# Zero fills and key conversions on ScalarE, and the order of issue as a literal list, in a linear-attention and long-convolution kernel

## The chip, the cores and the metric

The kernel runs on one core of a Trainium2 chip. A core has a tensor engine (PE, with its weight loads counted apart as PEld), a vector engine (DVE), a scalar engine (ACT), a GpSimd engine (POOL) and a sync engine (SP). Each takes the instructions of its own queue in the order in which they were issued; an instruction that waits holds up those behind it on its engine, and semaphores tie the engines together. Here POOL issues the loads that convert fp32 to bf16 on their way, and SP issues the plain copies, the transposing ones and the stores. The metric is the time of one execution on the device, in microseconds (us); less is better.

## The reference

Two computations follow each other. The first is linear attention with positive random features over 8 batches, 8 heads, 576 rows and 64 columns, with 128 features; the second is a gated long convolution over rows of 512 columns.

```python
def phi(x):                                   # x: q or k, times 1/sqrt(sqrt(64))
    h = einsum('bhsd,md->bhsm', x, omega) - sum(x * x, -1) / 2
    return exp(h - max(h, -1)) / sqrt(128)
q_p, k_p = phi(q_s), phi(k_s)
kv, z = einsum('bhsm,bhsd->bhmd', k_p, v), sum(k_p, axis=2)
attn = (q_p @ kv) / (q_p @ z + 1e-6)          # per batch and head

x = attn with the heads side by side           # 8 x 576 x 512
x1, x2, x3 = split(x @ w_proj)                 # w_proj 512 x 1536
conv = irfft(rfft(x2, axis=1) * rfft(filter_fft, axis=0), n=576)
out = (x1 * conv * x3) @ w_out                 # w_out 512 x 512
```

## The kernel before

**Staging.** The eight batches are worked in pairs. Of the 576 rows of a batch, 512 are the main part (4 tiles of 128) and 64 are "left" rows, which are handled for two batches at once (names ending in `l`). For each batch the keys are transposed on PE (or, from batch 5, by transposing copies on SP), multiplied by the features `om`, and put through the exponential on ACT (`ek`, `ekl`); they are then multiplied with the values (`vn`, for left rows `vcl`) into `kv`. The queries give `eqt` in the same manner. The product of `eqt` and `kv` holds numerator and denominator, and DVE divides (`rden`, `xb`). PE turns the result (`xt`, evicted by ACT) and DVE folds it along the sequence into `xf`.

The convolution of length 576 is done as a discrete Fourier transform split into three chunks of 192 rows, by matmuls with tables of sines. `project2` makes x2, `gates` (line 1250) makes x1 times x3, `forward` (1348) makes the spectrum with the tables `fwb`, `fwa`, `fwn`, `fwar` and `fwnr`, `spectrum` (1271) multiplies by the filter's spectrum `hps` and `hqs`, and the inverse (1411 and on) comes back with the tables `gtab`, `gta` and `gns`, to be added up and gated on DVE. Row halves that have to trade places go through SP copies (`sw`, `xw`). The product with `w_out` is evicted into `osb` and stored by SP in 256 KB pieces. The left rows of a pair have a gate of their own, `x13l`, made by DVE from a PE result that sits in one of the three banks of the PSUM tag `h`; the buffer `osb` has three slots, two half-sized evictions (`ya`) of the inverse also using them.

**The tables.** `make_residues` (599) makes the phases of the sines: constants by memset on DVE (`zb` holds zeros, `kc`, `ph`, `mg`), a first sine on `zb` that brings in the sine's table (`sn`), then for three sizes an activation on ACT (`yt`), a subtraction on DVE and a fused product that give the residue, whose sign bits are masked (`xt`). `sines` (668) puts them through the sine on ACT, `tables` (685) has PE transpose them, and DVE copies them out. `late_constants` (766) zeroes three buffers with DVE memsets and makes the scale `fsc`:

```python
for z in (hqs[:, 1, :], fwar[:], vcl_buf[1][:]):
    nc.vector.memset(z, 0.0)
```

**The first keys.** `first_keys` (510) has SP load the keys of batch 0 in two halves as fp32 (`ek`), and converts one half on DVE and one on ACT to bf16 (`kn`). Every other input comes by converting loads on POOL's queue: 76 of them, the projection weights (`wproj`) in three thirds of 512 KB, and a load of the next batch's keys, values or queries waits until the last reader of its buffer is done. The buffers for keys, values and queries are two deep (`kn`, `vn`, `qn`).

**What sets the order.** The whole kernel is recorded first: proxies for the engines make an `Op` of every call, consecutive matmuls into one tile being one `Op` (1348 in all). `Plan.order` (253) finds the dependences; the base time of an op is worked back from its users by latencies that `_cost` (200) gives, plus the tables `LEAD`, `SHIFT` and `LEAN` by stage, batch and engine (25 to 52). `simulate` (282) then plays the engines, the buffer slots, the load queues and PE's clock, and picks on each engine the ready op that is due first. `issue` (399) sends them all out in that order, so every instruction in the profile carries the line 405; they are told apart by tile names.

Of the kernel before, what the change touches and what calls it, by code (L numbers as in the profile page):

```python
# [24 lines left out]
PERIOD, STRETCH, STAY = 136.732, 16.038, 101.39  # L25
LEAD = {
    "cross keys": 0.92, "cross out": 7.64, "cross queries": -0.74, "filter": 4.65, "fold": -48.94,
    "forward": 107.85, "gates": -40.51, "inverse": 17.39, "keys": -0.75, "left keys": -52.95,
    "left out": -1.12, "left queries": -14.15, "load filter": 50.17, "load k": 55.36,
    "load kl": -1.11, "load q": -0.71, "load ql": 8.56, "load v": 0.49, "load vl": 1.73,  # L30
    "load w0": 1.61, "load w1": 5.28, "load w2": 1.64, "out": -42.88, "queries": 96.24,
    "residues": 1.41, "rest": 14.42, "sines": 0.5, "start": -189.65, "sums": -10.66,
    "tables": 0.2, "turn out": -3.18, "turn queries": 16.85, "values": -5.78, "zeros": 9.94,
}

SHIFT = {
    ("fold", 0): 48.94, ("fold", 1): 188.96, ("fold", 2): 50.05, ("fold", 7): 48.3,
    ("forward", 0): -112.16, ("forward", 1): -114.87, ("forward", 2): -107.32,
    ("forward", 6): -108.25, ("gates", 0): 16.24, ("gates", 1): 40.13, ("gates", 2): 50.94,
    ("gates", 6): 38.24, ("left keys", 2): 53.69, ("left keys", 6): 49.69, ("load k", 2): -56.64,  # L40
    ("load q", 0): -1.89, ("load ql", 0): -33.49, ("load v", 0): 2.07, ("load vl", 2): -6.7,
    ("queries", 1): -97.56, ("queries", 2): -131.03, ("queries", 6): -98.12,
    ("queries", 7): -93.75, ("rest", 1): 207.08, ("rest", 7): -14.42, ("turn out", 1): -12.03,
    ("turn out", 2): -153.32, ("turn queries", 1): -15.77, ("turn queries", 2): -16.64,
    ("values", 1): 546.29, ("values", 2): -24.51,
}
LEAN = {
    ("forward", "DVE"): 35.53, ("forward", "PE"): -40.96, ("gates", "DVE"): -10.03,
    ("gates", "PE"): 146.99, ("keys", "ACT"): -14.86, ("left queries", "ACT"): -47.8,
    ("queries", "ACT"): 5.49, ("queries", "PE"): 33.51, ("rest", "ACT"): -8.58,  # L50
    ("rest", "DVE"): -16.93,
}
# [33 lines left out]
class Op:  # L86
    __slots__ = (
        "eng", "calls", "reads", "writes", "due", "n", "busy", "lat", "deps", "users",
        "tiles", "start", "end", "name", "dma", "table", "where", "rows", "base",
    )  # L90

    def __init__(self, eng, due, n, name, where):
        self.eng, self.due, self.n, self.name, self.where = eng, due, n, name, where
        self.calls, self.reads, self.writes = [], [], []
        self.busy = self.lat = 0.0
        self.deps, self.users = {}, []
        self.tiles = set()
        self.dma = self.table = None
        self.rows = 128
# [13 lines left out]
class Plan:  # L113
# [4 lines left out]
    HOP = {"PE": 55.0, "DVE": 37.0, "ACT": 37.0, "POOL": 60.0, "SP": 60.0}  # L118

    def __init__(self, nc, tc):  # L120
        self.nc, self.tc = nc, tc
        self.ops, self.tile_of, self.slots = [], {}, {}
        self.where = "start", 0
        self.tensor = Proxy(self, "PE", nc.tensor)
        self.vector = Proxy(self, "DVE", nc.vector)
        self.scalar = Proxy(self, "ACT", nc.scalar)
        self.gpsimd = Proxy(self, "POOL", nc.gpsimd)
        self.sync = Proxy(self, "SP", nc.sync)
        self.allow_low_precision = nc.allow_low_precision
# [4 lines left out]
    def _new(self, eng, name):  # L134
        stage, b = self.where
        more = LEAD.get(stage, 0.0) + SHIFT.get((stage, b), 0.0) + LEAN.get((stage, eng), 0.0)
        op = Op(eng, more, len(self.ops), name, self.where)
        self.ops.append(op)
        return op

    def tile(self, pool, shape, dtype, name, bufs=1):
        t = pool.tile(shape, dtype, name=name, bufs=bufs)
        key = t.name if hasattr(t, "name") else t[:].tensor.name
        self.slots[pool.name, name] = bufs
        line = self.where[0]
        self.tile_of[key] = ((pool.name, name), "residues" if line == "load filter" else line)
        return t
# [7 lines left out]
    def record(self, eng, real, name, args, kw):  # L155
# [16 lines left out]
        if join:  # L172
            op = last
        else:
            op = self._new(eng, f"{name} {outs[0].tensor.name}")
            op.rows = ins[0].ap[0][1] if eng == "PE" else 128
# [5 lines left out]
        self._cost(op, eng, name, outs, ins)  # L182
        if name == "activation":
            op.table = {AF.Exp: "exp", AF.Sin: "sin"}.get(kw["func"])
        return op

    def opaque(self, eng, call, out, busy):
# [3 lines left out]
        op.busy = op.lat = busy  # L191

    @staticmethod
    def _free(ap):
        n = 1
        for _, c in ap.ap[1:]:
            n *= c
        return n

    def _cost(self, op, eng, name, outs, ins):  # L200
        out = outs[0]
        n = self._free(out)
        if name == "dma_start_transpose":
            op.busy, op.lat = 2000.0, 2200.0
            op.dma = ("HW", self._free(out) * 128 * 2 / 240.0)
            return
        if name == "dma_start":
            a = out if out.space != bass.MemoryType.DRAM else ins[0]
            run = a.ap[-1][1] * SIZE[a.dtype]
            rows = a.ap[0][1] * self._free(a) // a.ap[-1][1]  # L210
            if eng == "POOL":
                op.busy, op.lat = (880.0 if rows > 600 else 720.0), 3300.0
                op.dma = ("SW", rows * max(run, 166) / 198.0)
            elif out.space != bass.MemoryType.DRAM and ins[0].space == bass.MemoryType.DRAM:
                op.busy, op.lat = 580.0, 2300.0
                op.dma = ("HL", rows * run / 330.0)
            else:
                op.busy, op.lat = 580.0, 2000.0
                op.dma = ("HW", rows * run / 180.0 / (1 if out.space == bass.MemoryType.DRAM else 4))
            return  # L220
        half = all(SIZE[a.dtype] == 2 for a in (out, *ins))
        sbuf = all(a.space != bass.MemoryType.PSUM for a in (out, *ins))
        if eng == "PE":
            m = n / (4.8 if ins[0].ap[0][1] == 64 else 2.4) + 2.5
            op.lat = op.busy + n / 2.4 + 166.0
            op.busy += m
            return
        if eng == "DVE":
            if name == "memset":
                busy = n * SIZE[out.dtype] / 4.8 + 5.0  # L230
            elif name == "reciprocal":
                busy = 5.8 * n + 78.0
            elif name == "tensor_tensor":
                busy = n / (1.92 if half and sbuf else 0.96) + 68.0
            elif name == "scalar_tensor_tensor":
                busy = n / 0.96 + 130.0
            elif name in ("tensor_copy", "tensor_scalar", "tensor_scalar_mul"):
                rate = (4 if sbuf else 2) if half else (2 if sbuf else 1)
                if name != "tensor_copy" and not sbuf:
                    rate = 1  # L240
                busy = n / (0.96 * rate) + (68.0 if half else 100.0)
            elif name == "reduce_max":
                busy = self._free(ins[0]) / 0.96 + 60.0
            else:
                busy = n / 0.96 + 68.0
            op.busy, op.lat = busy, busy + 82.0
        elif eng == "ACT":
            busy = n * 0.8333 + (52.0 if not sbuf else 190.0)
            op.busy, op.lat = busy, busy + 107.0
        else:  # L250
            op.busy = op.lat = n / 1.2 + 100.0

    def order(self):
        last = {}
        for op in self.ops:
# [6 lines left out]
            for key, kind in ((op.reads, 0), (op.writes, 1)):  # L262
                for t, r in key:
                    last[t].append((op, kind, r))
                    if t in self.tile_of:
                        op.tiles.add(t)
        for op in self.ops:
            for o in op.deps.values():
                o.users.append(op)
        for op in reversed(self.ops):  # L270
            lat = op.lat + (op.dma[1] if op.dma else 0.0) + 50.0
            last = min((u.base for u in op.users), default=op.where[1] * PERIOD)
            op.base = last - STRETCH * lat / 1000.0
        for op in self.ops:
            op.due += op.base
            if op.eng == "PE":
                for u in op.users:
# [4 lines left out]
    def simulate(self):  # L282
# [8 lines left out]
        for op in ops:  # L291
            for t in op.tiles:
                left[t] = left.get(t, 0) + 1
# [1257 lines left out]
```

## Time and profile before

| | us |
|---|---|
| median of 5 runs (lowest, highest) | 267.3 (266.68, 268.03) |
| the profiled execution, own time | 269.08 |
| its span, first to last instruction | 267.0 |
| PE busy | 245.2 (92%) |
| DVE busy | 213.3 (80%) |
| ACT busy | 195.3 (73%) |
| POOL busy | 61.3 (23%) |
| mean granted PE clock | 0.987 |

A busy time is the sum over an engine's instructions. In the tables of stages that follow, an entry such as 5.83 (x58) is busy time and number of instructions. A line of the trace in order of time has the start, the length, the engine, the source line, the operation, output and input tile, their shapes and types, and the number of instructions that it joins; a bracket gives the idle time of the engine just before it and what ended that. Other groups of the page: POOL's 76 loads share one queue, which moved 16.78 MB, and SP's queue moved 19.04 MB.

### The profile page before, as it was taken

What the parts mean: (1) busy time and instruction counts of PE and PEld (TensorE: products, weight loads), DVE (VectorE), ACT (ScalarE), POOL (GpSimd) and SP (SyncE); (2) the same over time, 40 slices, a digit from 0 to 9 for tenths busy, and PEclk for the clock granted to TensorE, in tenths of its full rate; (3) what the DMA queues carried; (4) which work ended last, traced back from release to release, by engine and by line L of the source; (5) the groups of instructions that cost most, each with busy time, mean ns of one, the idle gap of its engine ahead of it and who ended that gap; (6) DMA issues with size and microseconds to landing.
All of it is one profiled execution on the core that took longest, in us unless ns stands there. A gap on an engine that the chain in (4) does not pass through costs nothing. (4 is left out here: it accounts for less than half of the span.)

```text
span 267.0 us, 5756 instructions
## 1 busy us (share of the span) xinstructions
PE 245.2 (92%) x2234; PEld 137.1 (51%) x2234; DVE 213.3 (80%) x475; ACT 195.3 (73%) x307; POOL 61.3 (23%) x86
## 2 busy tenths in 40 slices
PE   0586689999999999989999999999999999999994
PEld 0455446555476538545456454446555554456541
DVE  7999963689959999998499995979979789188470
ACT  5699479849999997986947876996495564753523
POOL 8625475444650710650031000000000000000000
PEclk9999959999999999999999999999999999999999
DMA  7999999999999999699869459525226410430406
GB/s 177 190 198 189 200 200 191 203 179 161 176 171 147 81 116 169 72 155 179 203 103 133 100 120 215 140 81 157 56 44 180 100 42 20 157 79 2 153 4 196
DMA packets 88866, 36.31 MB, mean 136 GB/s; under 512 B 60299, under 2 KB 83336, under 8 KB 88840
## 3 DMA queue, kind: packets, MB, share of 16 engines
q0 software_dynamic: 58560, 16.78, 60.9%
q1 hardware_dynamic: 30136, 19.04, 30.0%
q8 instruction: 17, 0.28, 0.4%
q10 hardware_dynamic: 144, 0.13, 0.1%
q14 instruction: 9, 0.07, 0.1%
HBM read 34.64 MB, written 9.44 MB: 165 GB/s over the span
## 5 line engine op out<-in xcount | busy, mean ns | idle before, releaser
L405 ACT CAST x<-h 128x512 bf16<-128x512 f32 x68 | 39.9, 597 | 31.2 <-PE h L405 28.2
L405 PE MATMUL h<-xt,wproj 128*128 128x512 bf16 x256 | 61.2, 380 | 0.0
L405 PEld LDWEIGHTS <-wproj 128*128 128x128 bf16 x384 | 31.2, 98 | 27.1 <-issue 2.1
L405 ACT ACTIVATE eqt<-a 128x1024 bf16<-128x1024 f32 x32 | 32.4, 1068 | 4.6 <-PE a L405 4.6
L405 ACT ACTIVATE osb<-h 128x512 f32<-128x512 f32 (+4 forms) x49 | 28.3, 577 | 8.0 <-PE h L405 6.6
L405 ACT ACTIVATE ek<-a 128x1024 bf16<-128x1024 f32 x32 | 32.3, 1048 | 0.7 <-PE a L405 0.6
L405 PE MATMUL h<-wproj,xf 128*128 128x512 bf16 x128 | 31.2, 379 | 1.2 <-DVE x13l L405 0.7
L405 PE MATMUL h<-wout,yt 128*128 128x512 bf16 x128 | 30.9, 379 | 0.3 <-DVE yt L405 0.3
L405 POOL DMA_DIRECT2D qn<-in_q_dram x26 | 22.9, 892 | 33.8 <-DMA qt<-qn 19.1
L405 DVE TENSOR_TENSOR x<-h,x 128x512 bf16<-128x512 f32 x32 | 21.8, 684 | 6.4 <-PE h L405 6.2
L405 DVE TENSOR_TENSOR bt<-h,osb 128x384 f16<-128x384 f32 x32 | 16.5, 552 | 7.8 <-PE h L405 5.3
L405 PEld LDWEIGHTS <-xf 128*128 128x128 bf16 x134 | 12.5, 99 | 14.1 <-issue 1.7
L405 PEld LDWEIGHTS <-yt 128*128 128x128 bf16 x128 | 11.9, 98 | 14.8 <-issue 0.9
L405 PE MATMUL h<-x,fwb 128*128 128x512 bf16 x72 | 18.5, 379 | 0.1
L405 PE MATMUL h<-gtab,xs 128*128 128x384 bf16 x64 | 15.6, 326 | 0.0
L405 PE MATMUL a<-om,kt 64*128 64x128 bf16 x256 | 12.1, 226 | 2.4 <-DVE kt L405 1.1
L405 PEld LDWEIGHTS <-eqt 128*128 128x128 bf16 x256 | 10.9, 98 | 5.7 <-DVE xb L405 1.3
L405 DVE TENSOR_TENSOR xb<-a,rden 128x512 bf16<-128x512 f32 x20 | 13.3, 684 | 0.4
L405 DVE TENSOR_TENSOR xf<-xt 128x1024 bf16<-128x1024 bf16 (+1 forms) x16 | 8.6, 550 | 6.3 <-ACT xt L405 6.3
L405 PE MATMUL a<-kv,eqt 128*128 128x65 bf16 x256 | 12.1, 194 | 1.0 <-DVE xb L405 1.0
L405 PE MATMUL a<-qt,om 64*128 64x512 bf16 x64 | 11.7, 397 | 1.0 <-ACT ek L405 0.7
L405 ACT CAST osb<-h 128x384 f16<-128x384 f32 x16 | 8.0, 501 | 5.9 <-PE h L405 5.3
(159 smaller groups left out, 475.7 us busy)
## 6 DMA issues: line engine op xcount, KB each, us to landing
out_dram<-osb SPq DMA_DIRECT2D x24, 256.0 KB, 2.3
vn<-in_v_dram POOLq DMA_DIRECT2D x8, 512.0 KB, 10.2
kn<-in_k_dram POOLq DMA_DIRECT2D x7, 512.0 KB, 8.7
qn<-in_q_dram POOLq DMA_DIRECT2D x24, 128.0 KB, 7.6
sw<-sp SPq DMA_DIRECT2D x16, 128.0 KB, 2.3
wproj<-in_moe_w_proj_dram POOLq DMA_DIRECT2D x3, 512.0 KB, 9.8
ek<-in_k_dram SPq DMA_DIRECT2D x2, 512.0 KB
qn<-in_q_dram POOLq DMA_DIRECT2D x2, 512.0 KB, 11.2
```

Of the source, the lines that this page charges most:

```text
L405: getattr(real, name)(*args, **kw)
```

## The change

Three things change in the code. The order of issue is no longer planned: the tables, the costs and the simulation are taken out, and `ORDER` lists the 1348 op numbers in the order in which they go out, with an assertion that no op precedes what it depends on. The two halves of the first keys are both converted on ACT. The three zeroed buffers are written on ACT by copies from the one-column tile of zeros, recorded right after the first sine, in place of the DVE memsets.

```diff
-PERIOD, STRETCH, STAY = 136.732, 16.038, 101.39
-LEAD = {
...
+ORDER = """
+    0 33 28 34 9 7 1 35 61 2 5 141 37 60 38 36 29 8 32 6 30 15 42 41 43 12 44 142 24 49 13 25 31
+    27 84 50 45 51 39 46 54 10 26 3 47 22 17 48 89 74 53 212 4 55 11 52 90 57 83 85 62 75 56 86 14
...
+    1338 1339 1343 1341 1342 1344 1345 1347 1346
+"""
...
     def order(self):
...
-        for op in self.ops:
-            op.due += op.base
...
-        return self.simulate()
-
-    def simulate(self):
...
+        order = [self.ops[int(n)] for n in ORDER.split()]
+        place = {op.n: i for i, op in enumerate(order)}
+        assert len(place) == len(order) == len(self.ops)
+        for op in order:
+            assert all(place[n] < place[op.n] for n in op.deps), "an instruction before its data"
+        return order
...
@@ first_keys
-            if g == 0:
-                nc.vector.tensor_copy(out=t_[:, hs], in_=k32[:, hs])
-            else:
-                nc.scalar.copy(out=t_[:, hs], in_=k32[:, hs])
+            nc.scalar.copy(out=t_[:, hs], in_=k32[:, hs])
@@ make_residues
         nc.scalar.activation(out=sn[:], in_=zb[:], func=AF.Sin)
+        nc.at("fills", 0)
+        for z in (
+            vcl_buf[1][:].rearrange("p j h d -> p (j h d)"),
+            hqs[:, 1, :],
+            fwar[:].rearrange("p j c -> p (j c)"),
+        ):
+            nc.scalar.copy(out=z, in_=zb[:].to_broadcast([P, z.shape[-1]]))
@@ late_constants
-        for z in (hqs[:, 1, :], fwar[:], vcl_buf[1][:]):
-            nc.vector.memset(z, 0.0)
```

The fills are 1056 columns (`vcl`), 512 (`hqs`) and 256 (`fwar`) of bf16. What the list says, against the order that the planner gave:

- **ACT** starts: first sine, fill `fwar`, fill `vcl`, `yt` of the second size, fill `hqs`, `yt` of the first size, second half of the third `yt`, one half of the key conversion, first sine of `gtab`, first half of the third `yt`, other half of the key conversion, two more sines for `gtab`, the sine for `gns`, the sine for `gta`, the exponentials. Before: first sine, `yt` of two sizes, one half of the key conversion, the third `yt`, three sines for `gtab`, those for `gns` and `gta`, the exponentials.
- **DVE** starts with the constants, now without the three memsets and the conversion. The mask `mk` comes forward to the other constants' end or goes back, in two pieces; the copies of sine tables `gns` (second) and two of the `xf` copies, and one piece of `fsc`, come behind the first `fwb` copy and ahead of the second key copy; the `fwar` copy comes later. The `x13l` product of the first pair is at place 202 of DVE's queue instead of 228.
- **PE** keeps its order but for swaps by up to four places. Ahead of the second batch of key products there is now a matmul of the filter transform; the third query group of batch 1 goes ahead of the turning of an output; the left queries' transposes come behind one more query product.
- **POOL**'s loads are in another order from the third one on. Before: first left keys, first queries, first values, keys 1, values 1, queries 1, left queries, left values, the middle third of `wproj`, keys 2, filter, keys 3, the other two thirds, left keys, values 2, and so on. After: left values (half), left keys, a filter piece, queries 0, left queries, keys 1, left keys of the next pair, values 0, filter pieces, left values, left queries, queries 1, keys 2, filter pieces, the first listed third of `wproj` (the first columns), values 1, `wout`, keys 4's place taken by keys of a later batch only once their buffer is free, and the middle and last thirds of `wproj` behind them.
- **SP**: the two halves of the first keys change places; the moves of filter rows into `hps` and `hqs` have another order, one of them behind the first `sw` copies; one store of a left output row goes behind a transposing copy of keys near 162 us, and single stores change places with neighbours.

## The prediction

> **What bounds the kernel now.** I read the page's forty slices first, then busy time by stage, then the first 15 us by instruction, then every wait of the tensor engine. The slices (tenths busy; PEclk is the granted clock):
>
> ```profile
> PE   0586689999999999989999999999999999999994
> DVE  7999963689959999998499995979979789188470
> ACT  5699479849999997986947876996495564753523
> PEclk9999959999999999999999999999999999999999
> ```
>
> TensorE (PE) is full from slice 7 on, and slice 6, around 36 us, holds a clock dip. By stage (start and end, length, then PE, weight loads, DVE, ACT and POOL busy with counts, clock, DMA share, GB/s):
>
> ```profile
> 0.00:15.00 15.00, 5.83 (x58) 4.52 (x60) 12.74 (x48) 10.21 (x15) 10.93 (x22) 1.00 1.15 185
> 15.00:33.00 18.00, 12.71 (x205) 8.93 (x202) 17.40 (x38) 13.62 (x18) 7.41 (x11) 0.99 1.45 196
> 33.00:45.00 12.00, 11.01 (x105) 6.38 (x104) 5.62 (x13) 9.79 (x15) 8.42 (x11) 0.73 1.45 195
> 45.00:267.00 222.00, 215.69 (x1874) 117.31 (x1873) 177.54 (x379) 161.67 (x262) 34.58 (x43) 1.00 0.83 125
> ```
>
> After 45 us PE is busy 97% of the time: only its listed waits can be won there. Before 33 us DVE is the full engine (17.40 of 18), fed by a chain through ACT. The start, where the three zero fills and the key conversion lie:
>
> ```profile
> 3.78 1.30 ACT L405 ACTIVATE yt<-x,mg,fs 128x384 f32<-128x384 f32 x2 [1.54 <-DVE ph L405]
> 5.50 1.04 ACT L405 CAST kn<-ek 128x1024 bf16<-128x1024 f32 x1 [0.42 <-DMA ek<-in_k_dram]
> 7.40 0.17 DVE L405 MEMSET fwar<- 128x128 uint32 x1
> 7.88 0.27 DVE L405 MEMSET hqs<- 128x256 uint32 x1
> 8.21 0.50 DVE L405 MEMSET vcl<- 128x528 uint32 x1
> 8.63 0.63 DVE L405 CAST kn<-ek 128x1024 bf16<-128x1024 f32 x1
> 11.00 0.46 ACT L405 ACTIVATE x<-xt,ph 128x192 bf16<-128x192 f16 x1 [2.04 <-DVE xt L405]
> 11.81 1.28 ACT L405 ACT_TABLE_LOAD   x1
> ```
>
> PE's waits, each in brackets before the instruction that it delayed:
>
> ```profile
> 30.59 0.43 PE L405 MATMUL a<-kv,eqt 128*128 128x65 bf16 x8 [1.01 <-DVE xb L405]
> 35.23 0.61 PE L405 MATMUL a<-om,kt 64*128 64x128 bf16 x8 [0.69 <-ACT eqt L405]
> 45.25 0.59 PE L405 MATMUL h<-wproj,xf 128*128 128x512 bf16 x2 [0.51 <-ACT osb L405]
> 118.60 0.59 PE L405 MATMUL h<-wproj,xf 128*128 128x512 bf16 x2 [0.70 <-DVE x13l L405]
> 151.69 0.24 PE L405 MATMUL h<-gta,sp 128*128 128x192 bf16 x1 [0.49 <-ACT osb L405]
> ```
>
> **What the Trainium skill says.** "ScalarE: Activation LUTs", "What ACT_TABLE_LOAD costs", prices an activation without pointer operands at 186 ns plus 0.833 ns a column, back-to-back ones overlapping by 93. The trace agrees: 1024 columns come to 1.039 us, the key conversion above took 1.04. The same page, "Table sets: the hidden batching unit", says that copy is in every table set, so fills between sine and exponential load no table; the trace agrees, its conversion at 5.50 lies between sine-set instructions and no load follows. "TensorE: Matmul & The Clock Gate", "What's actually happening", puts the clock on a free-running window of 3413 ns; the trace has half clock from 32.76 to 39.58 us, which is 6.83, two windows.
>
> **The change part by part.** *Fills and conversion.* DVE loses 0.17 + 0.27 + 0.50 + 0.63 = 1.57 us. ACT gains fills of 256, 512 and 1056 columns: by that price less overlap (estimates) 0.31, 0.52 and 0.97, together 1.80; with the conversion's 1.04 less 0.09 it is 2.75. ACT's waits before its exponential table are 1.54 + 0.42 + 2.04 = 4.00 us, so 2.75 fits, if it falls into them. Following both lists by hand: two fills fill the 1.54; the third, between two residue products, and the earlier second conversion push the last residue product so that DVE's next step, ready about 7.7, stalls to about 8.9: 1.2 us of the 1.57 gone. DVE reaches the left-key copy at 9.5 to 9.6 (9.62 now) and the sine at 11.00 moves to 10.95 to 11.0. The first exponential (13.11) stays: 0, bounds -0.3 and +0.5, the latter if the fills take their stand-alone price (three times 0.09, plus the 0.2 by which DVE's chain is short of slack).
>
> *DVE from 13 to 32 us.* In the list, two small copies of sine tables (0.25 and 0.20) and a constant (0.06) come behind the filter copy, ahead of the second keys and the first normalisations: +0.5. One filter copy there waits on PE by about 0.35, another goes later (-0.2). Bounds +0.25 and +0.65; I take +0.5, because PE waits for exactly this chain (1.01 at 30.59).
>
> *PE from 30 to 45 us.* A filter matmul (0.61) now precedes the key matmul that waited 0.69: -0.7. At 45.25 the projection waited 0.51 for an ACT eviction that held a bank; the filter evictions come earlier: -0.5. Against this the third query group goes ahead of the second turned output and will wait for an exponential's bank: +0.5. Sum -0.7, bounds -1.4 (stand-in costs nothing) and 0 (the filter matmul was work that filled another hole).
>
> *After 45 us.* DVE's left-row gate of the first pair ran at 117.87 though its matmul ended at 106.59, holding one of three banks; it moves 26 places up DVE's queue, to before the wait: -0.70. ACT's copy at 150.76 had waited for a row buffer until an output store landed; the list has that store behind the last cross-key transpose on SP and gives the copy another buffer, free since 147.0: -0.49. A left-query wait at 69.43 (0.17) has one more product ahead: -0.17. Sum -1.36, bounds -1.4 and 0, the latter where freed time only meets the next wait.
>
> *Loads and stores.* POOL's casting loads are reordered throughout. From 6 to 42 us they move about 190 KB per us, a half-megabyte load in 2.65. The largest move is the middle third of the projection weights, issued at 13.97 now, behind 3456 KB counted up to its own end; in the list 6592 KB. At that rate, from 6.2 with what is under way, it lands at about 41.1, plus the 1.2 by which a consumer's release trails its bytes (first left keys: bytes 6.94, PE released 8.08): 42.3, an estimate, against its first use at 45.25: 2.9 us of cover, cost nothing. If it is gone, each us goes one to one into PE. The last third comes about 45 for gates at 51; the second values 34.2 for 36.6. The third keys can't be issued before key 2's transposes let the buffer go (44.74; issued at 29.66 now): with the loads' 8.7 to landing 53.4, for 57.97. Keys 5 about 85 for 91.09. On SP the omega load and the two first key halves swap (both halves are now ACT's), filter rows move in another order, and a spectrum row move goes behind the forward swaps (70.55 to 71.65) for a read at 83.01; the reordered stores near 150 are counted above. Nothing else is priced.
>
> **Sum.** 0 + 0.5 - 0.7 - 1.36 = -1.56. It is made in the profiled execution, whose span is 267.0 and own time 269.08; the span happens to lie by the median of the runs, 267.3, so I take the difference off the median: 265.7.
>
> **Rivals.** *The weights come late* (slower). Their place in the load queue is doubled, and all loads share one queue at 195 GB/s, already without a gap from 15 to 45 us. For: only 2.9 us of cover on a 36 us extrapolation; 8% less rate uses it up. Against: the rate is steady at 185 to 196. It decides from a landing at 45 on; at 48, with the rest of the sum standing, 267.3 - 1.6 + 3 = 268.7; with two of the small gains lost to new waits, up to 271. PE would then show one long wait ahead of its first projection, released by a DMA.
>
> *The clock dip goes.* For: half of 6.83 us is at stake, 3.4, and the fill-in of the waits at 30 to 35 raises the activity that the clock follows. Against: +0.5 on DVE lengthens the idle stretch just before, and the window's phase is not the kernel's. The weights' landing at 42.3 caps it at 2.9: 265.7 - 2.9 = 262.8; half of it, 264.
>
> *It doesn't do what it says: order moves nothing.* The start cancels as worked out, and the waits removed reappear as others, since ACT or DVE evictions follow PE at one rate. For: 1.2 of 1.57 us vanish in the first nine. Against: PE's late waits each have a nameable cause. 267.3 - 0.8 to + 0.8.
>
> **How the numbers follow.** A measurement of this kernel tells about 0.3%, 0.8 us, from no change. Forecast, 265.0 to 266.5: 0.38. Dip gone, 262.8 to 264 and the space to the forecast: 0.18. Order moves nothing, 266.5 to 268.1: 0.18. Slower, 268.1 to 271: 0.26, a quarter because so many loads change place and the price of only the largest was followed to its end. So faster 0.56, same 0.18, slower 0.26. The range of eight in ten leaves out the bottom of the dip case (under 263.3, about 0.07) and the top of the slow one (over 269.0, about 0.13). The likeliest's own range is 265.0 to 266.5.
>
> **What would show it.** Right: two table loads on ACT before 13 us, three copies from a one-column source of about 0.40, 0.61 and 1.07 us, DVE waiting about 1.2 us for the residue product near 8 us; the first exponential within 0.3 us of 13.11; xb's wait at about 30 us longer by half a us; no waits of 0.70 and 0.49 near 118 and 151; PE busy time the same, with clock 0.73 from 33 to 45. Wrong: a first exponential past 13.6 (the fills lie on the path); a wait for projection weights before 46; a mean clock above 0.99; a PE wait over 0.5 us behind a DMA after 45, which means a load I gave slack to.

## The result, and the profile after

The changed kernel takes 267.95 us (median of 36 runs, 266.34 to 269.80) against 267.54 for the kernel before (71 runs, 266.68 to 269.08): ratio 1.0015, 95% interval 1.0003 to 1.0026. It is 0.4 us slower, inside the 0.3% called "no change" above. The forecast was 265.7.

By the span, from the first to the last instruction, the loss is larger: 266.15 at the median against 265.4 (128 runs of the kernel before, made beside the experiments). What an execution takes outside its span went the other way, from 2.1 to 1.8 us. Only the kernel before and experiments 4 and 12 have the 2.1; every other kernel here has 1.8, also 2 and 10, which keep the fills on VectorE. So these 0.3 us are not the fills' own; what they are, no run shows. A time below that is set against the kernel before has them in its favour, except in 4 and 12.

Two sentences above are loose. In the list of POOL's loads, keys 4 stand ahead of the middle and last thirds of `wproj` and, like every load, wait for their buffer; the prediction's "third keys" are those of batch 3, which keys 4 have overtaken. On SP the omega load stays first; only the two halves of the first keys change places.

The profiled execution of the changed kernel took 268.03 us, with a span of 266.3, close to its medians. The profile shown of before (269.08, span 267.0) lies 1.5 above those of its kernel, and its span lay by the median of the *times* only by chance. The slices of the changed kernel, in the order shown of before:

```profile
PE   0677789999999999999999989999999999999994
DVE  6799876689859799999499796978889679479380
ACT  8898498859989987987929956996585655753623
PEclk9998999999999999999999999999999999999999
```

and the stages:

```profile
0.00:15.00 15.00, 6.33 (x66) 4.86 (x67) 11.14 (x44) 13.18 (x20) 11.36 (x24) 1.00 1.23 184
15.00:33.00 18.00, 13.23 (x192) 9.30 (x189) 16.68 (x35) 13.21 (x16) 10.11 (x13) 0.91 1.42 198
33.00:45.00 12.00, 10.80 (x128) 6.79 (x128) 8.44 (x21) 11.89 (x19) 1.05 (x2) 1.00 1.34 206
45.00:267.00 222.00, 214.30 (x1853) 116.04 (x1851) 175.09 (x374) 158.89 (x258) 38.86 (x48) 1.00 0.84 124
```

In the first stage 1.60 us went from DVE and 2.97 came to ACT. The clock dip is here one window (0.91 in the second stage) and not two; and POOL, which in 33 to 45 us was busy for 8.42, now has 1.05 there and 38.86 after 45, where it had 34.58. Followed by the same matmuls, PE is 2.2 us ahead of the profile of before at its 49 us, and only 0.7 ahead at the end: 1.5 us are lost where no dip is in either profile.

The start, from the trace in order of time:

```profile
2.14 0.39 ACT L232 CAST fwar<-zb 128x256 bf16<-128x256 f32 x1
2.44 1.06 ACT L232 CAST vcl<-zb 128x1056 bf16<-128x1056 f32 x1
4.39 0.60 ACT L232 CAST hqs<-zb 128x512 bf16<-128x512 f32 x1
6.02 1.03 ACT L232 CAST kn<-ek 128x1024 bf16<-128x1024 f32 x1
8.05 1.03 ACT L232 CAST kn<-ek 128x1024 bf16<-128x1024 f32 x1
8.18 0.36 DVE L232 TENSOR_SCALAR yt<-yt 128x384 f32<-128x384 f32 x1 [1.12 <-ACT yt L232]
11.74 1.28 ACT L232 ACT_TABLE_LOAD   x1
13.04 1.02 ACT L232 ACTIVATE ekl<-a 128x1024 bf16<-128x1024 f32 x1
```

The fills cost 0.39, 0.60 and 1.06, DVE stalls 1.12 for the last residue product, and the first exponential comes at 13.04, where before it came at 13.11. PE's waits, to be set against the five of before:

```profile
31.14 0.43 PE L232 MATMUL a<-kv,eqt 128*128 128x65 bf16 x8 [0.31 <-DVE xb L232]
36.53 0.60 PE L232 MATMUL t<-ident,xb 128*128 128x128 bf16 x4 [0.49 <-ACT xt L232]
...
66.26 0.38 PE L232 MATMUL h<-x2l,fwar 128*128 128x512 bf16 x1 [0.37 <-ACT x2l L232]
72.76 0.20 PE L232 MATMUL a<-vcl,ekl 128*128 128x65 bf16 x1 [0.29 <-DVE vcl L232]
...
150.22 1.02 PE L232 MATMUL h<-xt,wproj 128*128 128x512 bf16 x4 [0.44 <-DVE bt L232]
154.21 1.04 PE L232 MATMUL h<-wproj,xf 128*128 128x512 bf16 x4 [0.67 <-DVE xf L232]
```

The waits of 0.70 at 118 and 0.49 at 151 are gone, as is the one at 45; others stand at 66, 73, 150 and 154. The one at 150 is not the new order's: the kernels of experiments 1 and 3, which have the old order there, wait 0.42 for the same `bt` at 149, and not at 151.

### The profile page after: what moved, and what is told of

Same layout as the page of the kernel before. It is cut to its first block, busy times and chain, and to the rows that moved or that the text cites. A ratio compares the mean times of both kernels' runs of the same rounds, so it can differ in the third digit from the quotient of the medians.

```text
span 266.3 us, 5720 instructions
## 1 busy us (share of the span) xinstructions
PE 244.7 (92%) x2234; PEld 137.0 (51%) x2234; DVE 211.3 (79%) x471; ACT 197.2 (74%) x311; POOL 61.4 (23%) x86
## 5 line engine op out<-in xcount | busy, mean ns | idle before, releaser
L232 ACT CAST x<-h 128x512 bf16<-128x512 f32 x68 | 39.3, 596 | 32.0 <-PE h L232 31.6
L232 ACT ACTIVATE eqt<-a 128x1024 bf16<-128x1024 f32 x32 | 31.6, 1042 | 4.4 <-PE a L232 4.4
L232 ACT ACTIVATE osb<-h 128x512 f32<-128x512 f32 (+4 forms) x49 | 27.2, 564 | 7.5 <-PE h L232 4.9
L232 PEld LDWEIGHTS <-xf 128*128 128x128 bf16 x134 | 12.2, 99 | 13.4 <-DVE xf L232 1.3
L232 POOL DMA_DIRECT2D kn<-in_k_dram x7 | 6.3, 901 | 24.7 <-PE t L232 13.9
L232 PE MATMUL a<-vc,ek 128*128 128x65 bf16 x256 | 11.8, 200 | 0.1
```

Of the source, the lines that this page charges most:

```text
L232: getattr(real, name)(*args, **kw)
```

## The experiments

The order is a list of instructions in both kernels, once that of before is written down; so each experiment is a list, with or without the fills on ScalarE. "Head" is what stands among the first 240 entries, to about 45 us. All kernels compute the whole reference. The kernel before had 267.56 or 267.57 us in each set.

**1 and 2. Head or tail.** Theory A: the head gains and the tail loses; B: all of it is the clock; C: the head loses.

```diff
 e1: fills and both conversions on ScalarE
-ORDER = new
+ORDER = new[:240] + [n for n in old if n not in new[:240]]
 e2: fills and one conversion on VectorE
-ORDER = old
+ORDER = old[:240] + [n for n in new if n not in old[:240]]
```

> The changed kernel's first 240 instructions (to about 45 us, with the fills and both conversions on ScalarE), then everything else in the order of before. Theory A (the new head gains about 1 us at equal clock and the new tail gives it back): 266.4 us, ratio 0.996. Theory B (the head gains nothing at equal clock, the 2.2 us of the profile are clock windows alone): 267.5, ratio 1.000. Theory C (the loss comes from the load order of the head): 268.5, ratio 1.004 or more.

> The kernel before up to its 240th instruction (about 45 us, zero fills and one conversion on VectorE as before), then everything else in the order of the changed kernel. Theory A (the new tail loses about 1.5 us): 269.0 us, ratio 1.006. Theory B (the tail is neutral): 267.5, ratio 1.000. My prediction's own sum for the tail (-1.36): 266.1, ratio 0.995.

Measured: e1 266.59 us, ratio 0.9962 (0.9945 to 0.9980); e2 269.43, ratio 1.0071 (1.0045 to 1.0098). A holds: the head is worth -1.0, the tail +1.9 (by the span -0.7 and +2.2). The tail costs 1.4 behind the new head (changed kernel less e1). In e1's execution, at full clock throughout, PE's first projection shows something else:

```profile
42.56 1.02 PE L230 MATMUL h<-wproj,xf 128*128 128x512 bf16 x4 [0.51 <-DMA wproj<-in_moe_w_proj_dram]
```

The middle third of the weights releases it at 42.56; the prediction had estimated 42.3. In this execution the weights hold the new head by 0.51. They do not always: in e10, with the same order and also at full clock, there is no wait:

```profile
42.26 1.02 PE L230 MATMUL h<-wproj,xf 128*128 128x512 bf16 x4
```

**3. The fills and the conversion alone**, in the order of before (`yt1` to `yt3` are the residue activations of the three sizes, `xt1` to `xt3` what DVE makes of them).

```diff
 ScalarE's part of the old order
-sn  yt1  yt2  kn(half 2)  yt3a yt3b  gtab gtab gtab ...
+sn  fwar vcl  yt1  hqs  yt2  kn(half 2)  yt3a yt3b  gtab  kn(half 1)  gtab gtab ...
```

> The order of before throughout, only with the three zero fills and the second key conversion on ScalarE (fills behind the first sine and between the first two residue activations, the conversion behind the first sine of the tables). By my prediction's first step: no change at the first exponential, within 0.3 us of 13.1, and 267.5 us, ratio 1.000. Rival (the 1.57 us taken off VectorE shorten the chain): exponential at 12 us, 266.5, ratio 0.996. Other rival (the fills lie on the path): exponential after 13.6, 268, ratio 1.002.

Measured: 266.45, ratio 0.9963 (0.9947 to 0.9979). My first step, worth nothing, is wrong in this order. ScalarE's trace:

```profile
7.05 0.98 ACT L230 ACTIVATE yt<-x,mg,fs 128x192 f32<-128x192 f32 x2 [0.52 <-DVE xt L230]
8.18 0.61 ACT L230 ACTIVATE gtab<-xt,ph 128x384 bf16<-128x384 f16 x1
8.70 1.03 ACT L230 CAST kn<-ek 128x1024 bf16<-128x1024 f32 x1
...
11.46 1.28 ACT L230 ACT_TABLE_LOAD   x1
12.76 1.02 ACT L230 ACTIVATE ekl<-a 128x1024 bf16<-128x1024 f32 x1
```

With the residue activations `yt3` ahead of the second conversion, DVE does not stall for them, and the exponential is 0.35 earlier than before. Of the measured 1.1, then, 0.35 are seen at the exponential and 0.3 lie outside the span; the rest, some 0.4, is within the interval (from -0.6) and is not traced to a place.

**4. The gate alone.**

```diff
 VectorE's part of the old order
-... xfl(832) h1(376) ... xf(830) x13l(736) ytl(747) ...
+... xfl(832) x13l(736) h1(376) ... xf(830) ytl(747) ...
```

> The kernel before with one instruction moved: the product x13l of the first pair, on VectorE at about 109 us instead of 117.9. By my prediction's step (wait of 0.70 at 118 goes): 266.8 us, ratio 0.9974. Rival (the freed time meets the next wait): 267.5, ratio 1.000.

Measured: 267.05, ratio 0.9979 (0.9962 to 0.9996), -0.5. The wait of 0.70 is gone, and two smaller ones have come:

```profile
110.58 1.02 PE L230 MATMUL h<-wproj,xfl 128*128 128x512 bf16 x4 [0.32 <-DVE x13l L230]
112.83 0.20 PE L230 MATMUL a<-vcl,ekl 128*128 128x65 bf16 x1 [0.36 <-DVE vcl L230]
```

Together they are 0.68, and yet there is a gain: e3 above and e11 below differ by this move alone, and their profiles are at full clock. In e11 PE is 0.59 us behind e3 at 110 us, by these two waits, and 0.57 ahead at 117, because the long wait and small ones near it are gone.

**5 to 8. Which engine's list makes the tail slow.** From the new waits I held VectorE's order to be the cause (A1); the rivals were ScalarE's, TensorE's, and the order of loads and transfers (A4). In each, one engine's part behind the head goes back to the order of before:

```diff
 e5, e6, e7, e8: the changed kernel, behind the first 240 entries
-VectorE | ScalarE | TensorE | POOL and SP: in the new order
+VectorE | ScalarE | TensorE | POOL and SP: in the old order
```

> The changed kernel with, behind its first 240 instructions (about 45 us), VectorE's instructions in the order of before; all other engines as changed. Theory A1 (the tail's loss is VectorE's order: waits for vcl 0.29 at 72, bt 0.44 at 150, xf 0.67 at 154 and small ones go, about 1.9 us, while the wait for the x13l gate of the first pair, about 0.5, comes back): 266.5 us, ratio to the kernel before 0.996. Rival (the loss is in what the other engines do): 268.4, ratio 1.003, since only the gate's gain is given up.

> The changed kernel with, behind its first 240 instructions, ScalarE's instructions in the order of before; all other engines as changed. Theory A1 (VectorE's order is the cause): only the wait for x2l (0.37 at 66) goes: 267.6 us, ratio 1.000. Rival A2 (ScalarE's evictions are the cause): 266.3, ratio 0.995.

> The changed kernel with, behind its first 240 instructions, TensorE's instructions in the order of before; all other engines as changed. Theory A1 (VectorE's order is the cause): no gain, 267.9 us or more, ratio 1.0015. Rival A3 (TensorE's swaps ask for results earlier than they come): 266.5, ratio 0.996.

> The changed kernel with, behind its first 240 instructions, POOL's loads and SP's transfers in the order of before; the compute engines as changed. Theory A1: no change, 267.9 us, ratio 1.0015. Rival A4 (keys and values loaded out of turn, or the stores, delay a consumer): 266.5, ratio 0.996.

| | us | ratio to before (95%) |
|---|---|---|
| e5, VectorE old | 268.16 | 1.0014 (0.9998 to 1.0030) |
| e6, ScalarE old | 269.09 | 1.0043 (1.0019 to 1.0066) |
| e7, TensorE old | 273.96 | 1.0227 (1.0202 to 1.0251) |
| e8, POOL and SP old | 266.22 | 0.9942 (0.9921 to 0.9963) |

Giving VectorE its old order gains nothing. e6 and e7 are worse than either parent, as I read it because an engine's list fits those of the others; e7 has new waits of 1.28 and 1.19. So a half-way kernel that doesn't get faster settles nothing, neither for its engine nor against it, and e5 to e7 leave the three suspects where they were. A half-way kernel that gets faster does tell: e8 gains 1.7 us on the changed kernel and is no slower than e1, which has the whole tail of before. So the loss lies with the loads and transfers (A4), and A1 falls by this. In the changed kernel the trace of POOL, SP and VectorE around the last new wait reads

```profile
137.34 2.63 POOL L232 DMA_DIRECT2D qn<-in_q_dram  x3 [14.24 <-DMA qt<-qn]
139.93 0.72 POOL L232 DMA_DIRECT2D vl<-in_v_dram  x1
140.61 2.67 POOL L232 DMA_DIRECT2D qn<-in_q_dram  x3
141.95 4.93 SPq L232 DMA_TRANSPOSE xt<-h  x1
152.21 0.42 DVE L232 TENSOR_TENSOR xf<-xt,xtl 128x512 bf16<-128x512 bf16 x1 [1.58 <-DMA xt<-h]
```

and in e8 the queue then holds three loads fewer, and VectorE does not wait:

```profile
137.82 3.51 POOL L230 DMA_DIRECT2D qn<-in_q_dram  x4 [14.98 <-DMA qt<-qn]
141.90 4.16 SPq L230 DMA_TRANSPOSE xt<-h  x1
150.49 0.41 DVE L230 TENSOR_TENSOR xf<-xt,xtl 128x512 bf16<-128x512 bf16 x1
```

The new list puts the first load of queries 7, which must wait 14.24 us for a buffer, ahead of a half of the left values and two pieces of queries 6. These had long been free to go (e9 below issues them at 122 to 125 without a wait), but POOL's queue is in order; so seven loads, not four, are released together at 137 and are under way when SP issues the transposing copy of the attention output of batch 4 at 142. From its issue to its landing the copy takes 10.2 us here and 6.4 in e8; VectorE waits for it, and PE behind VectorE.

**9 and 12. The three loads, taken away and added.** Theory D, with the three moved and nothing else:

```diff
 e9: POOL's part of the new order (op numbers)
-483 357 421 477 418 479 480 481 476 482 420 419
+483 357 421 477 418 476 420 419 479 480 481 482
 e12: POOL's part of the old order
-422 418 419 420 421 476 477 474 475 483 479 480 481 482
+422 418 421 477 474 475 483 479 480 481 476 482 420 419
```

> The changed kernel with three of POOL's loads moved (a half of the left values of pair 6 and two pieces of queries 6): ahead of the four query loads of batch 7, where they go out at about 123 us, instead of among and behind them at 140 to 143. Theory D (these three crowd the transposing copy of the attention output of batch 4, issued at 142, which then lands late and holds VectorE for 1.58 us and TensorE for 0.67): the wait on the copy goes, 266.7 us, ratio to the kernel before 0.997. Rival (the gain with all the old load and transfer order came from elsewhere in the queues): 267.9, ratio 1.0015.

> The kernel before with the same three loads late, among and behind the four query loads of batch 7 as in the changed kernel, at 138 to 143 us. Theory D (the loads alone make the copy late): VectorE waits for the transposing copy, 268.2 to 268.7 us, ratio 1.0025 or more. Rival (it takes the new order on VectorE as well): 267.55, ratio 1.000.

Measured: e9 266.98, ratio 0.9971 (0.9955 to 0.9986), 1.0 less than the changed kernel; the copy lands after 6.4 us, VectorE's `xf` starts at 149.78 without a wait and PE has none at 154. e12 272.63, ratio 1.0199 (1.0167 to 1.0230): 5.1 us slower than before, by three loads alone. The direction was expected, the size (about 1) was not. The profile of before:

```profile
141.94 5.31 SPq L405 DMA_TRANSPOSE xt<-h  x1
147.34 1.18 SPq L405 DMA_DIRECT2D out_dram<-osb  x2
150.76 0.48 ACT L405 CAST osb<-h 128x384 f16<-128x384 f32 x1 [0.94 <-PE h L405]
```

and of e12 (an execution of 274.5, the slowest of its six):

```profile
142.08 5.50 SPq L230 DMA_TRANSPOSE xt<-h  x1
147.67 1.18 SPq L230 DMA_DIRECT2D out_dram<-osb  x2
154.84 0.48 ACT L230 CAST osb<-h 128x384 f16<-128x384 f32 x1 [4.87 <-DMA out_dram<-osb]
155.76 0.25 PE L230 MATMUL h<-gta,sp 128*128 128x192 bf16 x1 [4.42 <-ACT osb L230]
```

In the order of before two output stores follow the copy on SP, and ScalarE needs the buffer that one of them empties. In e12 the copy lands 12.2 us after its issue, at 154.3 (8.3 before), and ScalarE gets its buffer at 154.8. So the copy's delay reaches ScalarE by way of the stores, and PE is held for 4.42 us; whether the stores waited behind the copy or were slowed by the loads themselves, no run separates. The clock falls after the stillness (stages of e12):

```profile
150.00:156.00 6.00, 1.58 (x12) 0.72 (x11) 2.15 (x6) 1.16 (x3) 0.00 (x0) 0.99 1.48 88
156.00:160.00 4.00, 3.89 (x15) 1.42 (x14) 2.72 (x8) 3.11 (x4) 0.00 (x0) 0.59 0.00 0
```

From 150 to 156 the DMA share is 1.48 (0.25 in the profile of before): the transfers run through the hole. So D is settled by taking the three loads away and by adding them. Their price is 5.1 us in the old order and 1.0 in the new one, in which those two stores go out 16 and 13 us later (at 163.2 and 160.5) and ScalarE does not wait for them.

**10. The new order without the fills on ScalarE.**

```diff
 VectorE's part of the new order; the fills leave ScalarE
-... xt1 yt3 xt2 ...
+... xt1 fwar hqs vcl kn(half 1) yt3 xt2 ...
```

> The order of the changed kernel throughout, with the three zero fills and one key conversion back on VectorE (together, ahead of the third residue subtraction, where VectorE waited 1.12 us). If the fills on ScalarE are worth in the new order what they were worth in the old one (1.1 us): 269.0 us, ratio 1.0055. If by my prediction's first step they are worth nothing: 267.9, ratio 1.0015.

Measured: 268.12, ratio 1.0015 (0.9999 to 1.0030), 0.17 from the changed kernel; first exponential at 13.20. In the new order the fills on ScalarE are worth nothing that can be told, as the prediction's first step had it. That the stall behind the conversion eats the gain is argued, not shown: e1 has the same stall of 1.12 and its exponential at 12.78. Nor is the new head's order worth nothing by itself: e10 and e2 have the same tail and both keep the fills on VectorE, and the new head makes e10 1.3 us faster (269.43 to 268.12). Fills on ScalarE or a new order of the head each gain about 1 us; both together gain no more (e1).

**11. The two gains together**, edits 3 and 4 in the order of before.

> The order of before with only the fills and both conversions on ScalarE and the x13l product of the first pair early on VectorE. If the two gains add: 267.55 - 1.1 - 0.5 = 265.95 us, ratio 0.994. If they overlap: 266.45, ratio 0.996.

Measured: 265.99, ratio 0.9943 (0.9927 to 0.9959), where 265.95 was expected. The gains add, and this beats both kernels: 1.6 us under the kernel before (0.3 of them outside the span), 2.0 under the changed one, with five instructions changed or moved.

## Why the prediction was wrong

**Start (0; right for the change, in part by luck).** Fills of 0.40, 0.61 and 1.07 were forecast, 0.39, 0.60 and 1.06 came; stall 1.2, came 1.12; exponential at 13.04. But the sine forecast for 10.95 to 11.0 came at 10.50, and only because the last sine then waited 0.32 for VectorE did the exponential stay; in e1, with the same head, it came at 12.78, just outside the bound of -0.3. And the zero holds only for this list: the same edits gain 1.1 us in the order of before (e3), against 0 in the new one (e10).

**DVE from 13 to 32 us (+0.5), wrong.** e1 and e3 both ran at full clock and differ in the order of the head; their exponentials stand at 12.78 and 12.76, and the matmul that waits for `xb` at 30.11 and 30.19. The three small copies cost nothing there.

**PE from 30 to 45 us (-0.7), mis-sized.** At full clock, from the matmul that waits for `xb` to the first projection, e3 takes 12.56 us, e10 with the new order 12.06, and e1 12.45 with its 0.51 for the weights in it: -0.5 where the weights are in time, -0.1 where they are not. The waits did not vanish: in e3 two for `eqt` (0.32 and 0.53) stand where the profile of before, in its dip, has the one of 0.69; in e1 0.47, 0.31 and 0.49 stand there. The head in all was put at -0.2 and gave -1.0 (e1).

**After 45 us (-1.36), the step that failed.** Its three waits did go. But the gate is worth 0.5 alone (e4), where 0.70 was put; the 0.49 is matched by the 0.44 at 150; new waits came; and the sum of the tail is +1.9 (e2), or +1.4 behind the new head. The error stands in two of my phrases: bounds of "-1.4 and 0", which left no room for a loss in the stage that is busy 97%; and, of loads and stores, "Nothing else is priced". I asked of each load whether it would be there for its own reader. I did not ask what it does to the transfers of another queue that run at the same time. Putting POOL's and SP's order back yields 1.7 us (e8), the three loads alone 1.0 (e9). Whether the other 0.7 is real is open: e8 had only 8 runs, at a mean clock of 0.995 against 0.991 in e9, and in the two profiles the way from PE's first projection to the matmul `h<-wout,yt` near the end is the same, 214.60 and 214.64 us. It is 215.99 in the changed kernel, and 214.22 and 214.40 with the old tail (e1, e3); the last 0.2 to 0.4 are not explained.

**Rivals.** "The weights come late" named the right queue and the wrong loads: the weights cost PE at most 0.83 (e7), 0.51 in e1, 0.43 in e8, and nothing in the changed kernel's profile. But the cover of 2.9 us was counted to 45.25, a start that the dip had made late; at full clock the old order starts there at 42.75 (e3). "The dip goes" was a matter of chance from run to run, in both kernels alike; this needs the runs sorted by their mean clock (before: the 128 runs beside experiments 1 to 12):

| mean clock | before: share, median span | changed: share, median span |
|---|---|---|
| 0.998 and over | 20%, 264.9 | 19%, 265.2 |
| 0.992 to 0.997 | 38%, 265.4 | 44%, 266.1 |
| under 0.992 | 41%, 265.6 | 36%, 266.9 |

At each clock the changed kernel has the longer span, by 0.3 to 1.3 us (by the time -0.1 to +1.0, with the 0.3 outside the span); that its profile is 0.7 us shorter than that of before is a difference of dips. "Order moves nothing" (266.5 to 268.1) is where the time fell, but as a sum: -1.0 in the head, +1.9 in the tail by experiments, which with their intervals of some 0.5 and 0.7 is compatible with the +0.4 measured. The two parts need not add exactly.

## What to carry to other kernels

In an in-order load queue, a load that must wait for its buffer turns everything behind it into a burst; put the loads that are free to go ahead of it, and look at what else uses the DMA engines at the moment of its release. When queues are reordered, price the transfers of the *other* queues (transposing copies, stores) and their readers, not only each load against its own. One profile is one draw of the clock: compare spans at equal mean clock before crediting a wait, and look at the time outside the span apart.

## What the runs showed of the hardware that was not expected

Three converting loads more (of 64, 128 and 128 KB) in flight moved the landing of a transposing copy. From issue to landing it took 6.4 to 8.3 us in the seven profiles with four loads, and 9.5 to 12.4 in six of the seven with seven loads. The exception is e6, with 7.0: there the copy was issued 6.1 us behind the first of the loads, and 4.1 to 4.7 in the six. Its reader on VectorE waited 0.80 (e10), 1.18 (e2), 1.58 (changed kernel), 1.78 (e5) and 2.08 (e7); in e10 PE did not wait in its turn, in the changed kernel 0.67. In e12 ScalarE waited 4.87 for a store that SP issued behind the copy. In e12's profile, after 4.4 us of an idle PE, the clock was 0.59 in the next 4 us.
